# A new order of work for the first chunks, and float32 scores for four units

## The chip, the cores and the metric

The kernel runs on one core of a Trainium2 chip. The metric is the device time of one execution in microseconds. The core has TensorE (matrix multiplies, PE in the profile, its weight loads PEld), VectorE (DVE), ScalarE (ACT), GpSimd (POOL) and SyncE (SP), which here issues every DMA. Each engine has its own stream of instructions, works through it in order, and waits for the others by semaphores.

## The reference

Causal attention with a window of 64 keys, batch 8, 8 heads, 576 positions, head dimension 64, and behind it a gated feed-forward layer over the 4608 tokens, 512 wide, with 2048 hidden units, in float32:

```python
scores = scale * np.matmul(q, k.transpose(0, 1, 3, 2))
mask = (rel >= 0) & (rel < window)
scores = np.where(mask, scores, -1000000000.0)
attn = np.exp(scores - np.max(scores, axis=-1, keepdims=True))
attn = attn / (np.sum(attn, axis=-1, keepdims=True) + 1e-09)
x = np.matmul(attn, v)                  # (4608, 512) after the heads are joined
h = x @ w_in
sp = np.maximum(h, 0.0) + np.log1p(np.exp(-np.abs(h)))
return (h * erf(sp)) @ w_out
```

`w_in` and `w_out` arrive in float64, 8 MB each, and are seen as pairs of int32.

## The kernel before

**Precision.** A float32 matrix is split into a float16 high part and a float16 rest, both scaled by a power of two, and a product is three float16 matmuls: high by high, high by rest, rest by high. The power of two comes from the largest exponent of the data: of q, k and v per chunk, of a weight per pair of tiles.

**Tiles.** The tokens form 36 *units* of 128 and 18 *chunks* of two units. The hidden layer is cut in two halves, so there are 36 *groups*, each one chunk with one half of the weights; `ORDER` (L42) says which, and before the change groups 0 to 3 are chunk 0 with both halves, then chunk 1 with both. The weights come in 16 raw tiles of 1 MB, 0 to 7 from `w_in`, 8 to 15 from `w_out`; tiles 0 to 3 and 8 to 11 belong to the first half. `SLOTS` (L44) says in which buffer a raw tile lands: two staging buffers, two buffers of the hidden layer, and the room of the second half of `w_out` (A, B) until its own values are written there.

**A unit of attention.** Load q, k, v (`lq`, `lk`, `lv`, L320 to L328); peaks of each (`pk`, L332); the chunk's scales, through two small matmuls (`pa pb px py pc`, L344 to L364); high parts and rests (`qh ql kh kl vh vl`); scores (`s`, L383: 48 matmuls of 64x64 weights); mask and row maximum on VectorE (`m`, L396), subtraction (`f`, L402), two exponentials per half of the heads on ScalarE (`e`, L406: one writes float16, one float32), the rest (`r`, L411); DMA transposes (`t`, L415); weighting of v (`a`, L418); division (`n`, L426); split (`xh`, `xl`) and transposes (`xt`) of the result.

**A weight tile.** Fetch (`L`, L464); from float64 to float32: low bits on VectorE (`d`, L474), re-biasing of the exponent on ScalarE (`c`, L478), assembly on VectorE (`o`, L482); largest value (`b`, L488); for a pair, the scale through small matmuls (`mb mx my mc`, L492 to L507) and a diagonal matrix of it (`dg`, L509); high part (`h`, L521); the rest either on VectorE (`l`, L525) or as a sum on TensorE, float32 weight by diagonal less the high part (`lp`, L531 and L532), narrowed by `le` (L438).

**A group.** Four blocks of 24 matmuls for the hidden layer (`mm`, L568), each evicted by `ev`; softplus and erf in two halves (`sp` L580, `er` L584), the product (`gt`, L588), its split (`gh`, `gl`), and the output's matmuls (`mA`, `mB`, L604), added up over the two halves in the buffer `ob` (`fo`, L607) and stored (`st`). Exponential, softplus and erf lie in different tables of ScalarE, and a change of table is an instruction (ACT_TABLE_LOAD).

**Order.** The whole program is one string, `PLAN` (L47 to L208). Each word is a call: `e:3:1` is the exponentials of unit 3, second half of the heads; a trailing `a`, `v` or `g` chooses ScalarE, VectorE or GpSimd. The words are called one after the other and nothing reorders them, so the string sets each engine's order and that of all DMA issues on SyncE. `wm:k:n` (L619) issues n matmuls of the identity into an unused corner of a PSUM bank; nobody reads them.

Of the kernel before, what the change touches and what calls it, by code (L numbers as in the profile page):

```python
# [41 lines left out]
ORDER = [(0, 0), (0, 1), (1, 0), (1, 1)]  # L42
ORDER = ORDER + [(c, hf) for c in range(len(ORDER) // 2, NCH) for hf in range(2)]
SLOTS = "S0 S1 A B h1 y1 S0 S1 A B S0 S1 S0 S1 S0 S1".split()  # L44

# [644 lines left out]
```

## Time and profile before

| | us |
|---|---|
| median of 3 runs | 951.34 |
| lowest, highest | 949.7, 952.21 |
| the profiled execution | 948.91 |
| its span, first to last instruction | 947.1 |
| TensorE busy, all matmuls | 907.8 |
| of it hidden layer (L568) | 393.3 |
| of it output (L604) | 262.5 + 136.5 |
| of it filling matmuls (L621) | 37.6 |

A profile is one execution. A row of a group of instructions reads: line, engine, operation, output <- input, shapes, count | busy time in all, mean of one in ns | idle time of the engine just before them, and what ended it. A row of the timeline starts with its start and its length in us. A row of the stretches gives the length, the busy time of each engine in it with the number of instructions, TensorE's granted clock as a share of full speed, the busy share of the DMA engines and GB/s.

### The profile page before, as it was taken

How to read it: one execution, taken by the hardware profiler on the slowest of the kernel's cores; microseconds unless marked ns; L12 is line 12 of the kernel's file. 1: busy time of each engine (PE TensorE's matmuls, PEld its weight loads, DVE VectorE, ACT ScalarE, POOL GpSimd, SP SyncE). 2: the span in 40 equal slices, each digit the busy share in tenths (PEclk: the TensorE clock that was granted, in tenths of full speed). 3: DMA queues.
4: the chain of work that ended last, by engine and by line, in shares of the span. 5: the costliest groups of instructions: out<-in, count | busy, mean ns of one | idle time of the engine just before them, and what ended most of it. 6: DMA issues, size and time to landing. Idle time of an engine off the chain costs nothing.

```text
span 947.1 us, 22314 instructions
## 1 busy us (share of the span) xinstructions
PE 907.8 (96%) x9344; PEld 607.6 (64%) x9344; DVE 669.0 (71%) x1521; ACT 639.3 (68%) x740; POOL 291.5 (31%) x262
## 2 busy tenths in 40 slices
PE   8879898899999999999999999999999999999998
PEld 7547566656666666676766666666666666676663
DVE  4877887889879878476868686868686767644232
ACT  5878958889587785384848484848575757574543
POOL 0222243522245441424252525252525252501000
PEclk9989899999999999999999999999999999999999
DMA  9675673433443642343333334343434342402000
GB/s 367 161 194 175 161 151 87 145 99 101 129 107 107 142 111 79 59 109 78 113 76 115 79 113 89 102 96 102 99 96 92 93 101 55 77 15 33 14 23 23
DMA packets 140533, 98.64 MB, mean 104 GB/s; under 512 B 117776, under 2 KB 117904, under 8 KB 140432
## 3 DMA queue, kind: packets, MB, share of 16 engines
q1 hardware_dynamic: 140432, 97.22, 40.5%
q8 instruction: 73, 1.20, 0.5%
q14 instruction: 28, 0.23, 0.1%
HBM read 59.44 MB, written 9.44 MB: 73 GB/s over the span
## 4 chain that ended last, share of the span: by engine, by line
PE 68%; DVE 14%; DMA 9%; ACT 6%; issue 2%; SPq 1%; POOL 0%; DVEq 0%; ACTq 0%
PE o L604 38%; PE hp L568 22%; DMA vr<-v_in 5%; PE av L423 4%; DVE vs L318 3%; DVE y L588 3%; PE s L390 3%; DMA kr<-k_in 2%; DVE peaks L339 2%; DVE ob L613 1%; PE av L621 1%; ACT stage L478 1%; PE o L531 1%; ACT p L408 1%; ACT sm L409 1%
## 5 line engine op out<-in xcount | busy, mean ns | idle before, releaser
L568 PE MATMUL hp<-xt,w 128*128 128x256 f16 x3456 | 393.3, 273 | 1.3 <-ACT h L311 1.3
L568 PEld LDWEIGHTS <-w 128*128 128x128 f16 x3456 | 335.9, 98 | 53.7 <-issue 2.0
L604 PE MATMUL o<-w,gh 128*128 128x512 f16 x1152 | 262.5, 381 | 0.7 <-ACT ob L311 0.3
L604 PEld LDWEIGHTS <-gh 128*128 128x128 f16 x1152 | 109.9, 98 | 125.6 <-issue 3.2
L311 ACT ACTIVATE h<-hp,c 128x512 f32<-128x512 f32 x76 | 51.4, 679 | 138.4 <-PE hp L568 138.3
L604 PE MATMUL o<-w,gl 128*128 128x512 f16 x576 | 136.5, 380 | 0.0
L318 DVE SCALAR_TENSOR_TENSOR gl<-y,sg,gh 128x1024 f16<-128x1024 f32 x72 | 93.1, 1294 | 26.3 <-PE o L604 24.0
L311 ACT ACTIVATE gh<-y,sg 128x1024 f16<-128x1024 f32 x67 | 76.7, 1145 | 48.2 <-DVE y L588 30.1
L404 POOL TENSOR_TENSOR sm<-sm,mx 128x512 f32<-128x512 f32 x41 | 46.5, 1138 | 189.1 <-DVE mx L399 188.2
L413 POOL TENSOR_TENSOR p<-sm,p 128x512 f16<-128x512 f32 x63 | 78.6, 1248 | 66.0 <-ACT sm L409 62.8
L588 DVE TENSOR_TENSOR y<-h,y 128x1024 f32<-128x1024 f32 x72 | 86.8, 1224 | 13.2 <-ACT y L584 13.2
L313 DVE TENSOR_SCALAR h<-hp,c 128x512 f32<-128x512 f32 x68 | 50.5, 744 | 55.8 <-PE hp L568 53.6
L446 POOL TENSOR_TENSOR xs<-x,xs 128x512 f16<-128x512 f32 x33 | 52.7, 1597 | 119.0 <-DVE xs L440 87.4
L604 PEld LDWEIGHTS <-gl 128*128 128x128 f16 x576 | 52.8, 98 | 54.8
L408 ACT ACTIVATE p<-sm,shift,cde 128x512 f16<-128x512 f32 x72 | 58.2, 808 | 36.5 <-POOL sm L404 32.4
L399 DVE CUSTOM_DVE_ANT_0 sm<-s,mask 128x128 f32<-128x128 f32 x288 | 65.0, 285 | 19.6 <-POOL p L413 10.5
L315 POOL TENSOR_SCALAR qs<-qr,csc 128x512 f16<-128x512 f32 x28 | 29.8, 1074 | 149.8 <-DVE csc L306 136.2
L580 ACT ACTIVATE y<-h 128x1024 f32<-128x1024 f32 x72 | 72.9, 1050 | 2.1 <-DVE gl L318 1.5
L584 ACT ACTIVATE y<-y 128x1024 f32<-128x1024 f32 x72 | 73.0, 1050 | 0.4
L409 ACT ACTIVATE sm<-sm,shift,cde 128x512 f32<-128x512 f32 x72 | 58.6, 814 | 2.4
L318 DVE SCALAR_TENSOR_TENSOR vs<-vr,csc,vs 128x1024 f16<-128x1024 f32 x36 | 54.0, 1527 | 3.0 <-POOL vs L315 3.0
L613 DVE SCALAR_TENSOR_TENSOR ob<-o,sg,ob 128x512 f32<-128x512 f32 x36 | 26.3, 745 | 41.9 <-PE o L604 41.8
(129 smaller groups left out, 984.1 us busy)
## 6 DMA issues: line engine op xcount, KB each, us to landing
vr<-v_in SPq DMA_DIRECT2D x36, 512.0 KB, 4.6
kr<-k_in SPq DMA_DIRECT2D x36, 384.0 KB, 3.7
qr<-q_in SPq DMA_DIRECT2D x36, 256.0 KB, 2.8
out<-ob SPq DMA_DIRECT2D x36, 256.0 KB, 2.3
stage<-w_out SPq DMA_DIRECT2D x6, 1024.0 KB, 5.3
stage<-w_in SPq DMA_DIRECT2D x4, 1024.0 KB, 5.4
w<-w_in SPq DMA_DIRECT2D x2, 1024.0 KB, 10.9
w<-w_out SPq DMA_DIRECT2D x2, 1024.0 KB, 6.7
```

What stands on the lines that cost most here:

```text
L311: nc.scalar.activation(dst, src, AF.Copy, scale=s)
L318: nc.vector.scalar_tensor_tensor(dst, src, s, hi, op0=ALU.mult, op1=ALU.subtract)
L399: nc.vector.tensor_tensor_reduce(smi(u, par)[:, j, :], sps[par][:, j, :], mask[:, var, :], 1.0, LOWEST, op0=ALU.add, op1=ALU.max, accum_ou ...
L408: nc.scalar.activation(pp[0][u % 2][:, HP * par:HP * par + HP, :], s, AF.Exp, bias=shift14, scale=es)
L409: nc.scalar.activation(s, s, AF.Exp, bias=shift14, scale=es)
L413: eng_of(eng).tensor_tensor(pp[1][u % 2][:, sl, :], smi(u, par), pp[0][u % 2][:, sl, :], op=ALU.subtract)
L446: eng_of(eng).tensor_tensor(xs[1][u % 2], x_flat(u), xs[0][u % 2], op=ALU.subtract)
L568: nc.tensor.matmul(hps[pc % 2][:, f, :], w1[a][:, cc, fs], xt[b][c % 2][:, cc, :], start=(n == 0), stop=(n == 3 * NCC - 1))
L580: nc.scalar.activation(at(yb, g, n), at(hb, g, n), AF.Softplus)
L584: nc.scalar.activation(y, y, AF.Erf)
L588: nc.vector.tensor_tensor(y, at(hb, g, n), y, op=ALU.mult)
L604: nc.tensor.matmul(ops[j], a[:, f, ts], w2[b][:, hf * GF + f, :], start=f == 0 and a is gh and b == 0, stop=f == GF - 1 and a is gl)
```

## The change

- `PLAN` is new up to chunk 8's first hidden blocks; behind that the engines' orders are those of before. There is no `wm` in it (570 matmuls less), and `warm` and the unused `table` are gone. The attention of unit 0 stands first, ahead of the weights.
- `ORDER`: groups 0 to 3 are now chunks 0 and 1 with the first half, then both with the second half. Weight tiles 0 to 3 and 8 to 11 are treated first, 4 to 7 and 12 to 15 later. Two output buffers (`ob`) hold the sums of chunks 0 and 1 meanwhile.
- `SLOTS` has two more places, C and D, in the room of `w_in`'s second half, where the tile lies in four pieces of 256 values (two DMAs), so the raw tile gets two more dimensions everywhere.
- Scores of units 0 to 3 are float32 matmuls of q and k as loaded, 16 instead of 48, with the constant 0.125 as the exponentials' scale. Their `qh ql kh kl` and the peaks of q and k are gone; v keeps its own.
- `mA` and `mB` are split by the output's 128 rows (a fourth field), the same matmuls in the same number.

```diff
-ORDER = [(0, 0), (0, 1), (1, 0), (1, 1)]
+ORDER = [(0, 0), (1, 0), (0, 1), (1, 1)]
-SLOTS = "S0 S1 A B h1 y1 S0 S1 A B S0 S1 S0 S1 S0 S1".split()
+SLOTS = "S0 S1 A B S0 S1 A B C D h1 y1 S0 S1 S0 S1".split()
+RAW = 4
+XT_BUFS, OB_BUFS = 2, 2
...
-    "wm:0:207 L:0 L:1 L:2 L:3 lq:0 lk:1 L:4 lm lv:0 lk:0 lq:1 lv:1 L:5 d:0 c:0 o:0 d:1 b:0:a c:1 d:2 o:1 c:2 b:1:a "
+    "lk:0 lq:0 lm s:0 lv:1 m:0:0 lq:1 lv:0 pk:1:2:v f:0:0:g e:0:0 L:0 m:0:1 f:0:1:g pk:0:2:v e:0:1 r:0:0:v lk:1 L:1 "
...
-    ob = ring("ob", 1, [P, TPC, DM])
+    ob = ring("ob", OB_BUFS, [P, TPC, DM])
...
     def scores(u):
+        terms = ((0, 0), (0, 1), (1, 0))
+        if u < RAW:
+            terms = ((None, None),)
         for i in range(HP):
-            for n, (a, b) in enumerate(((0, 0), (0, 1), (1, 0))):
+            for n, (a, b) in enumerate(terms):
+                qx, kx = (qr[u % 2], kr[u % 2]) if a is None else (qs[a][u % 2], ks[b][u % 2])
...
-                        nc.tensor.matmul(sps[par][t, i, :], qs[a][u % 2][rows, i, t],
-                                         ks[b][u % 2][rows, i, W * blk:W * blk + P], start=n == 0, stop=n == 2)
+                        nc.tensor.matmul(sps[par][t, i, :], qx[rows, i, t], kx[rows, i, W * blk:W * blk + P],
+                                         start=n == 0, stop=n == len(terms) - 1)
...
     def expo(u, par):
         s, es = smi(u, par), cde[u // TPC][:, 1:2]
+        if u < RAW:
+            es = 0.125
...
+    slots["C"], slots["D"] = (w1[n][:, :, DF // 2:].bitcast(I32).rearrange("p (a b) n -> p a b n", b=2) for n in range(2))
...
-    def mm2(g, n, terms):
+    def mm2(g, n, j, terms):
...
-    def warm(k, n):
-        for _ in range(n):
-            nc.tensor.matmul(idle, ident, ident[:, :120], start=True, stop=True)
```

How the change moves instructions, at three places. First SyncE, the head of its stream; `stage`, `w2` and `h1` are the places of raw weight tiles, `kr`, `qr`, `vr` the loaded k, q, v of even (0) and odd (1) units. Before:

```order
L470 DMA stage0_148<-w_in 128x2x1024
L470 DMA stage1_149<-w_in 128x2x1024
L470 DMA w2_0_139<-w_in 128x2x1024
L470 DMA w2_1_140<-w_in 128x2x1024
L321 DMA qr0_99<-q_in 128x512
L324 DMA kr1_102<-k_in 128x768
L470 DMA h1_142<-w_in 128x2x1024
L330 DMA mask_61<-mask_in 128x384
L327 DMA vr0_103<-v_in 128x1024
L324 DMA kr0_101<-k_in 128x768
```

and of the change:

```order
L338 DMA kr0_101<-k_in 128x768
L335 DMA qr0_99<-q_in 128x512
L344 DMA mask_61<-mask_in 128x384
L341 DMA vr1_104<-v_in 128x1024
L335 DMA qr1_100<-q_in 128x512
L341 DMA vr0_103<-v_in 128x1024
L495 DMA stage0_149<-w_in 128x2x1024
L338 DMA kr1_102<-k_in 128x768
L495 DMA stage1_150<-w_in 128x2x1024
L495 DMA w2_1_140<-w_in 128x2x1024
L436 DMA_TRANSPOSE pt0_0_124<-p0_0_120 128x8x128
```

k, q and v of units 0 and 1 have moved ahead of the weight tiles, and the first transpose of unit 0's weights (`pt`) now stands behind the third weight tile.

Second ScalarE, the head of its stream; L478 is the re-biasing of a weight tile, L488 its largest value, L337 a peak of k; in the change L428 and L429 are the exponentials, L503 the re-biasing, L325 here the high part of v, L513 the largest value. Before:

```order
L478 ACT_TABLE_LOAD
L478 ACTIVATE stage0_148<-stage0_148 128x1024
L488 ACTIVATE stage0_148,acc_63<-stage0_148 128x1024
L478 ACTIVATE stage1_149<-stage1_149 128x1024
L478 ACTIVATE w2_0_139<-w2_0_139 128x1024
L488 ACTIVATE stage1_149,acc_63<-stage1_149 128x1024
L337 ACTIVATE junk_84,peaks_62<-kr1_102 128x768
L478 ACTIVATE w2_1_140<-w2_1_140 128x1024
```

and of the change:

```order
L428 ACT_TABLE_LOAD
L428 ACTIVATE p0_0_120<-sm0_117,shift14_64 128x512
L429 ACTIVATE sm0_117<-sm0_117,shift14_64 128x512
L428 ACTIVATE p0_0_120<-sm1_118,shift14_64 128x512
L429 ACTIVATE sm1_118<-sm1_118,shift14_64 128x512
L503 ACTIVATE stage0_149<-stage0_149 128x1024
L503 ACTIVATE stage1_150<-stage1_150 128x1024
L325 ACTIVATE vs0_0_113<-vr0_103,csc_77 128x16x64
L325 ACTIVATE vs0_1_114<-vr1_104,csc_77 128x16x64
L513 ACTIVATE stage0_149,acc_63<-stage0_149 128x1024
L513 ACTIVATE stage1_150,acc_63<-stage1_150 128x1024
```

Four exponentials of unit 0 have moved to the front, where the first weight tile stood, and the peaks of k are gone.

Third ScalarE just ahead of its first instruction that serves the hidden layer (`h0<-hp`) in the program before, and ahead of the narrowing of the last weight sum that TensorE has queued before its first hidden matmul in the change. L438 (L458) with `w1_1` is a narrowing, with `xs` the attention's result. Before:

```order
L438 ACTIVATE xs0_1_130<-x0_128 128x512
L311 ACTIVATE qs0_1_106<-qr1_100,csc_77 128x512
L311 ACTIVATE qs0_0_105<-qr0_99,csc_77 128x512
L311 ACTIVATE vs0_1_114<-vr1_104,csc_77 128x16x64
L311 ACTIVATE vs0_0_113<-vr0_103,csc_77 128x16x64
L438 ACTIVATE w1_1_138<-o0_155 128x512
L478 ACTIVATE w2_1_140<-w2_1_140 128x1024
L438 ACTIVATE w1_1_138<-o1_156 128x512
L488 ACTIVATE w2_1_140,acc_63<-w2_1_140 128x1024
L311 ACTIVATE h0_141<-hp0_153,c1_89 128x512
```

and of the change:

```order
L513 ACTIVATE w1_1_138,acc_63<-w1_1_138 128x4x256
L428 ACTIVATE p0_0_120<-sm1_118,shift14_64 128x512
L429 ACTIVATE sm1_118<-sm1_118,shift14_64 128x512
L458 ACTIVATE w1_1_138<-o1_157 128x512
L503 ACTIVATE y1_144<-y1_144 128x1024
L458 ACTIVATE w1_1_138<-o0_156 128x512
L458 ACTIVATE w1_1_138<-o1_157 128x512
L503 ACTIVATE h1_142<-h1_142 128x1024
```

In the change re-biasings of `w_out` tiles (L503 on `y1`, `h1`) and exponentials stand between the narrowings; the one into `w1_1` from `o0` frees the buffer in which TensorE's last sum ahead of its first hidden matmul is made.

More of the change, by code (lines that the diff above doesn't have):

```diff
@@ L268, in window_attention_gated_ffn @@
     xs = [ring(f"xs{n}_", 2, [P, DM], F16) for n in range(2)]
-    xt = [ring(f"xt{n}_", 2, [P, NCC, CT], F16) for n in range(2)]
+    xt = [ring(f"xt{n}_", XT_BUFS, [P, NCC, CT], F16) for n in range(2)]
     w1 = ring("w1_", 2, [P, NCC, DF], F16)
@@ L283, in window_attention_gated_ffn @@
     wrow, wall = avb[:1, 1, row_at:row_at + P], avb[:, 1, row_at + P:row_at + P + 1]
-    idle = avb[:, 0, row_at + P + 3:row_at + P + 123]
     hps = [ps.tile([P, 2, CT], F32, name=f"hp{i}") for i in range(2)]
@@ L449, in x_turn @@
         c, j = divmod(u, TPC)
-        nc.sync.dma_start_transpose(out=xt[n][c % 2][:, :, j * P:(j + 1) * P], in_=xs[n][u % 2])
+        nc.sync.dma_start_transpose(out=xt[n][c % XT_BUFS][:, :, j * P:(j + 1) * P], in_=xs[n][u % 2])
     slots = {"h0": hb[0], "h1": hb[1], "y0": yb[0], "y1": yb[1], "S0": stage[0], "S1": stage[1]}
-    slots = {n: t.bitcast(I32) for n, t in slots.items()}
-    slots["O"] = None
-    slots["A"], slots["B"] = (w2[n][:, GF:].rearrange("p f e -> p (f e)").bitcast(I32) for n in range(2))
+    slots["A"], slots["B"] = (w2[n][:, GF:].rearrange("p f e -> p (f e)") for n in range(2))
+    slots = {n: t.bitcast(I32).rearrange("p (a b n) -> p a b n", a=2, b=2) for n, t in slots.items()}
+    slots["C"], slots["D"] = (w1[n][:, :, DF // 2:].bitcast(I32).rearrange("p (a b) n -> p a b n", b=2) for n in range(2))
     def raw_tile(u):
@@ L460, in raw @@
     def raw(u):
-        r = raw_tile(u).rearrange("p (n w) -> p n w", w=2)
-        return r[:, :, 0], r[:, :, 1]
+        r = raw_tile(u).rearrange("p a b (n w) -> p a b n w", w=2)
+        return r[:, :, :, :, 0], r[:, :, :, :, 1]
     def fetch(u):
@@ L469, in fetch @@
             src = w_out[2 * (u - 8) * P:2 * (u - 7) * P, :]
-        nc.sync.dma_start(raw_tile(u).rearrange("p (a b) -> p a b", a=2), src.rearrange("(c p) f -> p c f", p=P))
+        dst = raw_tile(u)
+        if SLOTS[u] in "CD":
+            for a in range(2):
+                nc.sync.dma_start(dst[:, a], src[a * P:(a + 1) * P, :].rearrange("p (b f) -> p b f", b=2))
+        else:
+            nc.sync.dma_start(dst.rearrange("p a b n -> p a (b n)"), src.rearrange("(c p) f -> p c f", p=P))
     def low_bits(u):
@@ L489, in bound @@
         else:
-            nc.vector.tensor_reduce(dst, lo, axis=AX.X, op=ALU.max, apply_absolute_value=True)
+            nc.vector.tensor_reduce(dst, lo, axis=AX.XYZ, op=ALU.max, apply_absolute_value=True)
     def pair_rows(j):
@@ L512, in parts @@
         j = u // 2
-        t = raw(u)[0].bitcast(F32).rearrange("p (c n) -> p c n", c=2)
+        t = raw(u)[0].bitcast(F32)
         if u < 8:
@@ L519, in parts, with quarters @@
         return t, sw2[:, j - 4:j - 3], hi, lo
+    def quarters(x):
+        return x.rearrange("p c (b n) -> p c b n", b=2)
     def high(u, eng):
         t, s, hi, _ = parts(u)
-        scaled(eng, hi, t, s)
+        scaled(eng, quarters(hi), t, s)
     def low(u):
         t, s, hi, lo = parts(u)
-        rest(lo, t, s, hi)
+        rest(quarters(lo), t, s, quarters(hi))
     def low_sum(u, a):
         t, _, hi, _ = parts(u)
-        nc.tensor.matmul(ops[a], diag[u // 2 % 2], t[:, a], start=True, stop=False)
+        nc.tensor.matmul(ops[a].rearrange("p (b n) -> p b n", b=2), diag[u // 2 % 2], t[:, a], start=True, stop=False)
         nc.tensor.matmul(ops[a], minus, hi[:, a], start=False, stop=True)
@@ L567, in mm1 @@
                 for a, b in ((0, 0), (0, 1), (1, 0)):
-                    nc.tensor.matmul(hps[pc % 2][:, f, :], w1[a][:, cc, fs], xt[b][c % 2][:, cc, :], start=(n == 0),
+                    nc.tensor.matmul(hps[pc % 2][:, f, :], w1[a][:, cc, fs], xt[b][c % XT_BUFS][:, cc, :], start=(n == 0),
                                      stop=(n == 3 * NCC - 1))
@@ L595, in g_lo @@
         rest(glb[:, sl], at(yb, g, n), st_g[g][:, n:n + 1], ghb[:, sl])
-    def mm2(g, n, terms):
+    def mm2(g, n, j, terms):
         hf = ORDER[g][1]
         gh, gl = (t.rearrange("p (f t) -> p f t", t=CT) for t in (ghb, glb))
-        for j in range(TPC):
-            ts = slice(j * P, (j + 1) * P)
-            for f in range(n * GF // 2, (n + 1) * GF // 2):
-                for a, b in (((gh, 0), (gh, 1)) if terms == 0 else ((gl, 0),)):
-                    nc.tensor.matmul(ops[j], a[:, f, ts], w2[b][:, hf * GF + f, :],
-                                     start=f == 0 and a is gh and b == 0, stop=f == GF - 1 and a is gl)
+        ts = slice(j * P, (j + 1) * P)
+        for f in range(n * GF // 2, (n + 1) * GF // 2):
+            for a, b in (((gh, 0), (gh, 1)) if terms == 0 else ((gl, 0),)):
+                nc.tensor.matmul(ops[j], a[:, f, ts], w2[b][:, hf * GF + f, :],
+                                 start=f == 0 and a is gh and b == 0, stop=f == GF - 1 and a is gl)
     def result(g, j, eng="v"):
@@ L617, in store @@
         nc.sync.dma_start(out[r0:r0 + P, :], ob[c % len(ob)][:, j, :])
-    def warm(k, n):
-        for _ in range(n):
-            nc.tensor.matmul(idle, ident, ident[:, :120], start=True, stop=True)
-    def table(n):
-        nc.scalar.preload_act_table_set(("exp_and_others", "softplus", "sigmoid_and_others")[n])
     HANDLERS = {
@@ L632, in window_attention_gated_ffn @@
         "W": w_in_scale, "V": w_out_scale, "dc": descale, "gn": gains, "mm": mm1, "ev": hidden,
-        "sp": softplus, "er": erf, "gt": gate, "gh": g_hi, "gl": g_lo, "mA": lambda g, n: mm2(g, n, 0),
-        "mB": lambda g, n: mm2(g, n, 1), "fo": result, "st": store, "T": table, "wm": warm,
+        "sp": softplus, "er": erf, "gt": gate, "gh": g_hi, "gl": g_lo, "mA": lambda g, n, j: mm2(g, n, j, 0),
+        "mB": lambda g, n, j: mm2(g, n, j, 1), "fo": result, "st": store,
     }
```

329 rows, old and new, of the table PLAN are left out of this document.

## The prediction, made before the changed kernel was run

> **What bounds the kernel now.** I read the busy table first, then the busy time of each engine in stretches, then the timeline of TensorE.
>
> ```profile
> PE 907.8 (96%) x9344; PEld 607.6 (64%) x9344; DVE 669.0 (71%) x1521; ACT 639.3 (68%) x740; POOL 291.5 (31%) x262
> ```
>
> The span is 947.1 us and TensorE is busy for 96% of it, so over the whole program it is the bound. That figure contains the filling matmuls, so the next view cuts the span at three matmuls that stand out in the timeline: the first hidden-layer matmul (71.32), the first of group 4, which is chunk 2 with the first half of the weights (163.60), and the third pair of group 16, chunk 8 (476.49).
>
> ```profile
> 71.32 5.40 PE L568 MATMUL hp<-xt,w 128*128 128x256 f16 x48
> 163.60 5.42 PE L568 MATMUL hp<-xt,w 128*128 128x256 f16 x48
> 476.49 2.79 PE L568 MATMUL hp<-xt,w 128*128 128x256 f16 x24
> ```
>
> ```profile
> core 0: us, PE busy (x) PEld busy (x) DVE busy (x) ACT busy (x) POOL busy (x), PEclk, DMA share, GB/s
> 0.00:71.32 71.32, 56.34 (x767) 41.17 (x768) 49.00 (x119) 50.26 (x70) 15.55 (x30) 0.95 0.77 240
> 71.32:163.60 92.28, 80.80 (x958) 58.90 (x955) 72.92 (x170) 74.80 (x98) 29.35 (x27) 0.94 0.55 139
> 163.60:476.49 312.89, 309.31 (x3153) 202.67 (x3145) 248.99 (x579) 226.35 (x258) 112.61 (x95) 1.00 0.43 108
> 476.49:947.10 470.61, 461.37 (x4486) 304.87 (x4478) 298.05 (x655) 287.92 (x316) 133.95 (x110) 1.00 0.32 74
> ```
>
> The same stretches for the filling matmuls (L621) alone, PE first:
>
> ```profile
> 0.00:71.32 71.32, 32.90 (x519) 30.80 (x519) 0.95 0.77 240
> 71.32:163.60 92.28, 4.66 (x54) 3.99 (x51) 0.94 0.55 139
> ```
>
> The ledger of TensorE up to 476.49 is then: busy 56.34 + 80.80 + 309.31 = 446.45, of it filler 32.90 + 4.66 = 37.56, so **408.9 us of work**, and 476.49 - 408.9 = **67.6 us without work** (48 before the first hidden matmul, 16 up to 163.60, 4 after). From 163.60 on it hardly waits. In the first 163.6 us ScalarE is busy for 125 and VectorE for 122, three quarters of it: the weights' conversion and the first attention units run through these two, and TensorE waits for their chain.
>
> Behind 476.49 the two kernels have the same instructions in the same order on TensorE (only the two row halves of one group's output are named apart), so the 470.6 us that follow stay. The question is how much of the 67.6 us goes.
>
> **The change part by part.** *Work removed and added.* Four units lose the float16 split of q and k and its peaks: on VectorE eight residuals and four peaks, on ScalarE four peaks and most of the scalings.
>
> ```profile
> L318 DVE SCALAR_TENSOR_TENSOR ks<-kr,csc,ks 128x768 f16<-128x768 f32 x36 | 41.6, 1186 | 0.1
> L318 DVE SCALAR_TENSOR_TENSOR qs<-qr,csc,qs 128x512 f16<-128x512 f32 x36 | 26.8, 775 | 0.1
> L339 DVE TENSOR_REDUCE peaks<-qr 128x1 f32<-128x512 f32 x31 | 20.7, 679 | 0.9 <-DMA qr<-q_in 0.9
> L580 ACT ACT_TABLE_LOAD x40 | 51.3, 1283 | 4.3 <-DVE cpw L360 3.6
> ```
>
> 4 x (1.186 + 0.775 + 0.679) = 10.6 us leave VectorE. ScalarE gains: its order now has 122 table loads for 105, 17 x 1.283 = 21.8 us, nearly all before chunk 8. By counts times these rows, ScalarE has some 11 us more ahead of the cut at 476.49, where it was idle for 125 us; it is hidden as long as ScalarE is not the late one, which it is only up to chunk 1 (below).
>
> *The float32 scores.* No score in float32 is in the trace. A float32 matmul of 512 columns is (L531), and a float16 one (L604), and the float16 scores (L390):
>
> ```profile
> 160.48 1.07 PE L531 MATMUL o<-stage,diag 128*128 128x512 f32 x2
> 161.39 0.38 PE L532 MATMUL o<-w,minus 128*128 128x512 f16 x1
> 122.40 0.86 PE L390 MATMUL s<-ks,qs 64*64 64x128 f16 x48
> 123.20 3.63 PE L604 MATMUL o<-w,gh 128*128 128x512 f16 x16
> 126.76 0.86 PE L390 MATMUL s<-ks,qs 64*64 64x128 f16 x48
> ```
>
> 161.39 - 160.48 = 0.91 us against (126.76 - 123.20) / 16 = 0.22: 4.1 times. 48 float16 score matmuls took 0.80; 16 in float32 at 4.1 times are 1.1 us if the four 64x64 corners still run side by side, and 16 x 0.91 / 4 = 3.6 us if they do not. Per unit +0.3 to +2.8, for four units +1 to +11. I take **+2**, near the scores' own row; all four stand ahead of the first hidden matmul or just there, where TensorE waits anyway. If that cover is gone it costs the whole.
>
> *The first stretch.* Now the loads of weights go first, and k waits behind them; the first softmax exponential starts at 36.79.
>
> ```profile
> 3.75 0.50 SPq L324 DMA_DIRECT2D kr<-k_in  x1
> 16.49 0.84 ACT L337 ACTIVATE junk<-kr 128x768 uint8<-128x768 f32 x1 [2.40 <-DMA kr<-k_in]
> 36.79 0.81 ACT L408 ACTIVATE p<-sm,shift,cde 128x512 f16<-128x512 f32 x1
> kr<-k_in SPq DMA_DIRECT2D x36, 384.0 KB, 3.7
> ```
>
> After the change k and q of unit 0 are the first two loads: at 3.7 us behind an issue at about 1 they land near 5, the scores end near 7, two masked maxima and a shift follow, and the first exponential starts near 10. From there ScalarE has, ahead of what the first hidden matmul needs, 6 pairs of exponentials, 7 re-biasings (L478), 6 bounds (L488), 2 scalings of v, 2 of weights, 4 narrowings (L438) and 2 diagonals:
>
> ```profile
> L408 ACT ACTIVATE p<-sm,shift,cde 128x512 f16<-128x512 f32 x72 | 58.2, 808 | 36.5 <-POOL sm L404 32.4 <-DVE sm L404 3.9
> L409 ACT ACTIVATE sm<-sm,shift,cde 128x512 f32<-128x512 f32 x72 | 58.6, 814 | 2.4
> L478 ACT ACTIVATE stage<-stage 128x1024 f32<-128x1024 f32 x10 | 11.4, 1138 | 3.9 <-DMA stage<-w_in 3.9
> L488 ACT ACTIVATE stage<-stage 128x1024 f32<-128x1024 f32 x9 | 10.4, 1157 | 4.5 <-DVE stage L482 4.4
> L488 ACT ACTIVATION_READ_ACCUMULATOR stage<-stage 128x1 f32 x9 | 1.8, 199 | 0.0
> L311 ACT ACTIVATE vs<-vr,csc 128x1024 f16<-128x1024 f32 x4 | 4.4, 1136 | 0.0
> L311 ACT ACTIVATE w<-stage,sw 128x1024 f16<-128x1024 f32 x4 | 4.8, 1212 | 0.0
> L438 ACT ACTIVATE w<-o 128x512 f16<-128x512 f32 x14 | 8.1, 596 | 1.6 <-PE o L532 1.6
> L509 ACT ACTIVATE diag<-unit,sw 128x128 f32<-128x128 f32 x8 | 3.2, 398 | 2.9 <-DVE sw L306 2.9
> ```
>
> 6 x 1.62 + 7 x 1.14 + 6 x 1.36 + 2 x 1.14 + 2 x 1.21 + 4 x 0.60 + 2 x 0.40 = 33.7 us. VectorE has 34 of its own. So nothing starts before 10 + 33.7 = 44, and the two hand work to each other in order: a weight tile goes VectorE, ScalarE, VectorE, ScalarE, and followed by hand through the rows above ScalarE stands three times before a re-biasing whose low-bits step is queued on VectorE behind attention (2 + 1 + 4 us), the last just ahead of the narrowing (the third piece of order in the section on the change) that the first hidden matmul waits for. With smaller gaps the first hidden matmul comes at **53 us**. Ends: 43 without a wait; 58 where ScalarE is busy for the same 70% (50.26 of 71.32) as before. TensorE's work ahead of it: now 56.34 - 32.90 = 23.4 with as many low-part sums and scores a few tenths longer, but one sum less per weight tile still open: 21. So **without work 53 - 21 = 32** (22 to 37) for 48.
>
> *First hidden matmul to chunk 1's (group 1).* ScalarE has in this part of the order 5 re-biasings, 4 bounds, 6 narrowings, 2 pairs of exponentials, 3 hidden evictions, 2 softplus and 2 erf, each with a table load, and 7 smaller pieces:
>
> ```profile
> L311 ACT ACTIVATE h<-hp,c 128x512 f32<-128x512 f32 x76 | 51.4, 679 | 138.4 <-PE hp L568 138.3
> L580 ACT ACTIVATE y<-h 128x1024 f32<-128x1024 f32 x72 | 72.9, 1050 | 2.1 <-DVE gl L318 1.5
> ```
>
> 5.7 + 5.4 + 3.6 + 3.2 + 2.0 + 4 x (1.05 + 1.28) + 6.6 = 36 us, of which some 4 us are not needed for group 1's first matmul. In these 31 us TensorE has 26 of work (4 hidden blocks at 5.42 / 2, 6 weight sums at 1.1, 4 weighings at 0.5, 3 quarter blocks of the output at 1.8, small ones): 5 without work (2 to 14). From there to the cut TensorE has work at every step I followed up to group 2; but VectorE, 80% busy between 163.60 and 476.49 (248.99 of 312.89), gets work that was done earlier: by counts times rows it is 82 us between the starts of groups 4 and 8, or 77, since such a sum over the whole program stands 7% above the 669.0 of the busy table; TensorE needs 83 there, so VectorE is at 93%. I take 7 without work (4, as now, to 14, that is 77 / 0.80 = 96 less 83). Together 12 for 20.
>
> *The filler.* It leaves 37.6 us of busy time that were no work, so its going costs nothing by itself. What it covered is the clock. TensorE's granted clock (the column behind POOL) falls when it was idle:
>
> ```profile
> 60.00:64.00 4.00, 1.12 (x16) 0.80 (x15) 2.65 (x12) 2.02 (x3) 2.59 (x3) 1.00 1.23 281
> 64.00:68.00 4.00, 2.72 (x17) 1.57 (x18) 2.89 (x9) 2.38 (x4) 1.60 (x2) 0.55 0.34 66
> 68.00:72.00 4.00, 4.00 (x17) 2.02 (x16) 3.07 (x5) 3.30 (x5) 0.00 (x0) 0.59 0.10 10
> 72.00:76.00 4.00, 4.00 (x39) 3.60 (x37) 1.96 (x3) 1.12 (x2) 0.00 (x0) 1.00 0.92 362
> ```
>
> After 4 us with 1.12 busy the clock is 0.55, and it is back after some 4 us of busy time. Without filler TensorE has 21 us of work in 53, so it will mostly run at about 0.55 there. Most of that stretches work into waits; on the chain are a few sums and the first hidden matmuls: 4 us at 0.57 lose 3. I take **+3** (0 to 20; the 408.9 already hold the slow stretches of now).
>
> The Trainium skill, in "TensorE: Matmul & The Clock Gate", Part 1, says the same as a rule that speaks against this change: a window of about 3.4 us without activity halves the clock, and another busy one is needed to restore it. The trace agrees (0.55 behind 1.12 busy in 4.00); taken over the whole first 100 us it is the last rival below, and by the 3 us above it would only be paid once or twice.
>
> *SyncE.* The transposes of the first units now stand between weight loads, which so wait for the first exponentials (about 15 us); the loads ahead of that point are 5.7 MB, 24 us at the first stretch's 240 GB/s, so the DMA engines are not out of work before. The second output buffer (`ob`) frees the accumulation from its store; no wait of TensorE in the page is put down to a store, so 0.
>
> **The sum.** 408.9 + 2 (scores) + 32 + 12 + 3 (clock) = 457.9 for 476.49: **18.6 us less**. The profiled execution took 948.91 (1.8 around its span): 930.3. The median of the runs shown is 951.34, 2.4 above it, so 932.7; I say **932 us**.
>
> **The rivals.** *It goes better*: ScalarE and VectorE hardly wait for each other. Then the low ends hold: 408.9 + 1 + 22 + 6 + 0 = 437.9, and the time is 951.34 - 38.6 = 913. For it: four units need no chunk scale ahead of their scores, and the second halves of the weights are not due before group 2, so each engine has more to choose from. Against: in the first 163.6 us ScalarE has held no more than 125. **0.20.**
>
> *It is only moved*: in-order queues give the gain back, since softplus and erf of chunks 0 and 1 and the second halves of the weights now meet in the same stretch with chunk 2 and 3's attention. With the high ends of the waits, 37 + 14 + 14, and the clock's 3: 408.9 + 2 + 65 + 3 = 478.9, the time 954; with one of them a little lower no change, 943 to 954. For it: VectorE's 93% between groups 4 and 8. **0.13.**
>
> *The clock stays down*, which ends slower. Place: from the first hidden matmul to group 2, about 51 us of TensorE's work, with short gaps by weight sums. If the gaps keep the granted clock at 0.57 there, it takes 51 / 0.57 - 51 = 38 longer, of which the 5 of waiting hide some: 457.9 + 33 = 491, the time **966**. It decides from a mean clock below 51 / (51 + 18.6 + 5) = 0.68 in that stretch; at 0.8 it costs 8 and the change is still faster. Against: between 71.32 and 163.60, with 4.66 of filler, the clock was 0.94. **0.10.**
>
> **How the numbers follow.** Forecast 0.57, better 0.20, moved 0.13, clock 0.10. A measurement of this kernel tells about 0.3%, 2.9 us, from no change. Faster: 0.57 + 0.20 + 0.05 of the third = 0.82; same 0.06; slower 0.10 + 0.02 = 0.12. The forecast's own range is 918 to 943; to leave out no more than 2 in 10 the range reaches down to the better case, 910, and up to the third, 950.
>
> **What would show it.** First exponential near 10 us and first hidden matmul near 53 (43 to 58); TensorE without work before it about 32 us; first matmul of group 1 near 85; the third pair of group 16 near 458, and 470 us behind it. A granted clock near 0.55 before 55 us and above 0.8 from there to 110. Wrong would be: a first hidden matmul later than 65, TensorE idle for over 10 us between groups 4 and 8 behind VectorE, or score matmuls of over 3 us a unit.

## The result, and the profile after

| | before | after |
|---|---|---|
| median of 4 runs each, us | 951.78 | 918.64 |
| lowest, highest, us | 949.7, 952.39 | 916.71, 918.84 |
| profiled execution, us | 948.91 | 918.84 |
| its span, us | 947.1 | 917.1 |

The ratio is 0.9651, with a 95% interval of 0.9631 to 0.9671: 33 us, 3.5%, faster. The forecast said 932, between 910 and 950; the direction and the range held, and the gain came out larger than its 19 us.

The busy table of the changed kernel:

```profile
PE 872.6 (95%) x8710; PEld 574.7 (63%) x8710; DVE 673.4 (73%) x1513; ACT 647.7 (71%) x738; POOL 274.0 (30%) x251
```

TensorE's share is lower by one point although the kernel is faster: 37.6 us of filler are gone from it. What counts is again the time without work, so here is the same cut. (The 16 float32 score matmuls of a unit are recorded as 32.) The timeline of TensorE gives the places: the first scores, the first hidden-layer matmul, that of group 1 (now chunk 1 with the first half), and the row that holds the third pair of group 16 as its second half.

```profile
4.64 1.99 PE L408 MATMUL s<-kr,qr 64*64 64x128 f32 x32 [4.64 <-DMA qr<-q_in]
...
39.99 1.10 PE L408 MATMUL s<-kr,qr 64*64 64x128 f32 x32
...
47.84 5.72 PE L596 MATMUL hp<-xt,w 128*128 128x256 f16 x48
...
75.94 5.74 PE L596 MATMUL hp<-xt,w 128*128 128x256 f16 x48 [0.28 <-DMA xt<-xs]
...
438.65 5.40 PE L596 MATMUL hp<-xt,w 128*128 128x256 f16 x48
```

24 such matmuls take 2.62 from start to start (484.50 - 481.88 further on), so the cut lies at 438.65 + 2.62 = 441.27. The stretches (length, busy time of PE, PEld, DVE, ACT, POOL, granted clock, DMA share, GB/s); 161.51 is a hidden-layer matmul of group 4:

```profile
0.00:47.84 47.84, 22.17 (x259) 12.70 (x260) 35.66 (x122) 34.24 (x47) 18.14 (x31) 0.97 1.04 315
47.84:161.51 113.67, 109.72 (x969) 67.55 (x967) 100.40 (x181) 98.48 (x121) 42.70 (x35) 1.00 0.50 143
161.51:441.27 279.76, 277.35 (x3014) 189.07 (x3007) 236.96 (x565) 223.68 (x250) 74.25 (x67) 1.00 0.45 107
441.27:917.10 475.83, 463.40 (x4480) 305.34 (x4477) 300.36 (x649) 291.29 (x322) 138.91 (x120) 0.99 0.33 78
```

Up to the cut TensorE is busy for 22.17 + 109.72 + 277.35 = 409.24 us, all of it work, and without work for 25.67 + 3.95 + 2.41 = 32.0, where it was 67.6. The cut comes 476.49 - 441.27 = **35.2 us earlier**. Behind it the same instructions take 475.83 instead of 470.61: **5.2 us are given back**. 35.2 - 5.2 = 30.0 is the difference of the two spans (947.1 - 917.1); the medians differ by 3 more.

### The profile page after: what moved, and what is told of

The parts are those of the page before. It is cut to its first block, busy times and chain, and to the rows that moved or that the text cites. A ratio compares the mean times of both kernels' runs of the same rounds, so it can differ in the third digit from the quotient of the medians.

```text
span 917.1 us, 20949 instructions
## 1 busy us (share of the span) xinstructions
PE 872.6 (95%) x8710; PEld 574.7 (63%) x8710; DVE 673.4 (73%) x1513; ACT 647.7 (71%) x738; POOL 274.0 (30%) x251
## 4 chain that ended last, share of the span: by engine, by line
PE 66%; DVE 16%; DMA 9%; issue 3%; ACT 2%; POOL 1%; SPq 1%; DVEq 0%; POOLq 0%; ACTq 0%
PE o L631 34%; PE hp L596 25%; DMA vr<-v_in 5%; DVE vs L332 3%; PE av L443 3%; DVE y L616 2%; PE s L408 2%; DVE peaks L353 2%; DVE sm L417 1%; DMA stage<-w_in 1%; DMA w<-w_out 1%; DMA w<-w_in 1%; PE o L559 1%; DVE gl L332 1%; DVE sm L422 1%
## 5 line engine op out<-in xcount | busy, mean ns | idle before, releaser
L631 PE MATMUL o<-w,gh 128*128 128x512 f16 x1152 | 265.9, 381 | 0.7 <-ACT ob L325 0.5
L631 PE MATMUL o<-w,gl 128*128 128x512 f16 x576 | 139.8, 380 | 0.2 <-DVE gl L332 0.2
L325 ACT ACTIVATE h<-hp,c 128x512 f32<-128x512 f32 x82 | 55.3, 677 | 104.0 <-PE hp L596 103.8
L332 DVE SCALAR_TENSOR_TENSOR gl<-y,sg,gh 128x1024 f16<-128x1024 f32 x72 | 95.4, 1326 | 19.2 <-PE o L631 17.8
L433 POOL TENSOR_TENSOR p<-sm,p 128x512 f16<-128x512 f32 x54 | 68.8, 1276 | 83.7 <-ACT sm L429 79.1
L422 POOL TENSOR_TENSOR sm<-sm,mx 128x512 f32<-128x512 f32 x37 | 42.7, 1156 | 170.8 <-DVE mx L417 170.8
L325 ACT ACTIVATE gh<-y,sg 128x1024 f16<-128x1024 f32 x55 | 62.9, 1144 | 40.2 <-DVE y L616 30.8
L428 ACT ACTIVATE p<-sm,shift,cde 128x512 f16<-128x512 f32 x64 | 51.9, 810 | 42.5 <-POOL sm L422 29.8
L327 DVE TENSOR_SCALAR h<-hp,c 128x512 f32<-128x512 f32 x62 | 45.9, 744 | 47.1 <-PE hp L596 46.6
L466 POOL TENSOR_TENSOR xs<-x,xs 128x512 f16<-128x512 f32 x27 | 40.9, 1516 | 109.1 <-DVE xs L460 49.5
```

What stands on the lines that cost most here:

```text
L325: nc.scalar.activation(dst, src, AF.Copy, scale=s)
L327: nc.vector.tensor_scalar(dst, src, s, None, op0=ALU.mult)
L332: nc.vector.scalar_tensor_tensor(dst, src, s, hi, op0=ALU.mult, op1=ALU.subtract)
L422: eng_of(eng).tensor_tensor(s, s, m.unsqueeze(2).broadcast_to([P, HP, P]), op=ALU.subtract)
L428: nc.scalar.activation(pp[0][u % 2][:, HP * par:HP * par + HP, :], s, AF.Exp, bias=shift14, scale=es)
L433: eng_of(eng).tensor_tensor(pp[1][u % 2][:, sl, :], smi(u, par), pp[0][u % 2][:, sl, :], op=ALU.subtract)
```

## The experiments

Twelve kernels were run, each beside runs of the kernel before on the same chip; these gave medians of 951.1 to 951.4, beside the change 951.78, so the times below are set side by side. In what follows "end" is the difference of medians; the interval of a ratio is about 0.002 on either side, so differences under 3 us between two of these kernels don't settle anything alone.

### The parts of the change, one at a time

**Before without its filler.** All `wm` words are left out, nothing else.

```diff
-    "wm:0:207 L:0 L:1 L:2 L:3 lq:0 lk:1 L:4 lm lv:0 lk:0 lq:1 lv:1 L:5 d:0 c:0 o:0 d:1 b:0:a c:1 d:2 o:1 c:2 b:1:a "
+    "L:0 L:1 L:2 L:3 lq:0 lk:1 L:4 lm lv:0 lk:0 lq:1 lv:1 L:5 d:0 c:0 o:0 d:1 b:0:a c:1 d:2 o:1 c:2 b:1:a "
```

> The kernel before with its 570 filling matmuls taken out and nothing else changed. My theory: the filler is no work and its going frees nothing, but it kept TensorE at full clock; without it the weight sums, scores and the first hidden matmuls up to about 100 us run at half speed, so the time is 3 to 10 us longer, first hidden matmul near 74 to 80 us. Rival (the changed kernel gains by losing the filler's 37.6 us of TensorE time): 5 to 35 us shorter. Rival (the clock is worth nothing there): within 2 us.

Measured: 946.89 for 951.17, ratio 0.9948 (0.9932 to 0.9965), 4.3 us **faster**. The theory fell, and the number lies between the two rivals. Its stretch up to the first hidden matmul, and that matmul:

```profile
0.00:69.24 69.24, 30.57 (x249) 12.95 (x249) 49.62 (x118) 49.28 (x69) 14.43 (x30) 0.83 0.75 246
69.24 5.40 PE L566 MATMUL hp<-xt,w 128*128 128x256 f16 x48
```

The clock did fall (0.83 for 0.95), and TensorE's work grew from 23.4 to 30.6 us; yet the first hidden matmul comes 2.1 us earlier than 71.32. So the stretched work lies mostly in waits, while a filling matmul that stands in TensorE's order ahead of work whose data are there holds it up. The timeline of before has one such place just at the end, five fillers ahead of a first hidden matmul that waits for nothing else; they are 0.46 of the 2.1 us:

```profile
70.86 0.62 PE L621 MATMUL av<-ident 128*128 128x120 bf16 x5
71.32 0.93 PE L568 MATMUL hp<-xt,w 128*128 128x256 f16 x7
```

Which of the 570 held up what was not tried one by one. The two spans (947.1 and 943.6) differ by 3.5 us, 1.9 of it at the cut; the other 1.6 arise behind it, where neither kernel has filler.

**The changed kernel with filler.** 278 of the same matmuls in nine places where TensorE waits (`warm` is put back), for instance

```diff
-    "lk:0 lq:0 lm s:0 lv:1 m:0:0 lq:1 lv:0 pk:1:2:v f:0:0:g e:0:0 L:0 m:0:1 f:0:1:g pk:0:2:v e:0:1 r:0:0:v lk:1 L:1 "
+    "lk:0 lq:0 lm wm:0:40 s:0 lv:1 m:0:0 lq:1 lv:0 pk:1:2:v f:0:0:g e:0:0 L:0 m:0:1 f:0:1:g pk:0:2:v e:0:1 r:0:0:v "
```

> The changed kernel with 278 filling matmuls put into the waits of TensorE in the first 46 us, each some 80% of the wait it stands in. If the clock was the cost there: float32 scores of units 0 to 2 take 1.1 us instead of 2.0, the first weight sums 0.9 instead of 1.9, the first hidden matmul comes 1 to 4 us before 47.84, and the time is 1 to 4 us shorter. If the half speed only stretched work into waits: within 1 us. If filler behind which other work queues is late: 1 to 3 us longer.

Measured: 922.51, ratio 0.9702 (0.968 to 0.9725), 3.9 us **slower** than the change. The third expectation came, a little larger. The first scores are quick now, but start later, and so does the first hidden matmul:

```profile
5.99 1.10 PE L409 MATMUL s<-kr,qr 64*64 64x128 f32 x32
...
49.18 5.72 PE L597 MATMUL hp<-xt,w 128*128 128x256 f16 x48
```

In both orders filler costs about 4 us at the end, whatever it saves in clock, and the change gains by leaving it out. How the loss comes about is shown only in part: here 1.3 of the 5.1 us between the spans are there at the first hidden matmul, and the rest arises behind the last filler.

**Float32 scores in the old order.** A first attempt left the loads of q and k of unit u+2 ahead of unit u's scores, so that these read q and k of a later unit and waited for their load.

> The kernel before with float32 scores for units 0 to 3, their splits and the peaks of q and k left out, order otherwise as it was. My theory: what the float32 scores are worth is that unit 0 no longer waits for a chunk scale, and that only pays where attention stands first; in the old order some 10 us of VectorE and 7 us of ScalarE work go, of which a part is on the chain: 2 to 7 us shorter. Rival (the work removed is the gain): 10 to 18 us shorter. Rival (nothing, it is hidden): within 2 us.

Measured: 951.88, ratio 1.001 (0.9992 to 1.0028). Since the scores waited for loads that they don't need, it settles nothing; in the second attempt the loads stand behind the scores:

```diff
-pc:0 lp:1:0 wm:5:35 d:5 qh:0:a qh:1:v kh:0:a ql:0 c:5 kl:0 lq:2 ql:1 s:0 wm:6:34 lk:2 o:5
+pc:0 lp:1:0 wm:5:35 d:5 c:5 s:0 lq:2 wm:6:34 lk:2 o:5
...
+        if u < 4:
+            terms = ((None, None),)
```

> The kernel before, in its old order, with one part of the change: the first four units' scores come from float32 q and k, so that the peaks and the float16 splits of q and k of those units are gone, and the load of unit u+2's q and k stands behind unit u's scores. Theory (the order carries the gain; in the old order the splits lie beside weight work that the first hidden matmul waits for anyway): 2 to 7 us shorter than before, first hidden matmul 2 to 6 us earlier than the 71 of before. Rival (the removed VectorE and ScalarE work is itself the gain): 10 to 18 us shorter. Rival (float32 scores are worth nothing): within 2 us.

Measured: 952.68, ratio 1.0019 (1.0004 to 1.0034). Nothing is gained, which is the second rival. The stretch up to its first hidden matmul:

```profile
0.00:70.75 70.75, 56.03 (x736) 41.94 (x736) 40.45 (x106) 43.97 (x58) 12.54 (x28) 0.90 0.75 242
```

VectorE has 8.6 us less in it than before (40.45 for 49.00) and ScalarE 6.3 less (43.97 for 50.26), and TensorE's first hidden matmul moves by 0.57. So in the old order neither engine's amount of work set that place.

**The change without float32 scores for units 0 and 1.** Their peaks, scales and float16 splits are back, their loads first:

```diff
-    "lk:0 lq:0 lm s:0 lv:1 m:0:0 lq:1 lv:0 pk:1:2:v f:0:0:g e:0:0 L:0 m:0:1 f:0:1:g pk:0:2:v e:0:1 r:0:0:v lk:1 L:1 "
+    "lk:0 lq:0 lk:1 lq:1 lv:0 lv:1 lm L:0 L:1 L:3 pk:0:1:a pk:0:0:v pk:1:1:a pk:1:0:v pk:0:2:v pk:1:2:v pa:0 pb:0 "
+    "px:0 py:0 pc:0 qh:0:a kh:0:v ql:0 kl:0 s:0 m:0:0 f:0:0:g e:0:0 m:0:1 f:0:1:g e:0:1 r:0:0:v d:0 c:0 c:1 qh:1:a "
...
-        if u < RAW:
+        if 1 < u < RAW:
```

> The changed kernel, but units 0 and 1 go back to float16 halves of q and k with a chunk's scale (peaks, scale, splits and three matmuls a block), their loads first. Theory (the float32 scores buy the early start of the exponentials): first exponential at 16 to 20 us instead of 8.7, first hidden matmul 6 to 10 us later, the end 6 to 10 us later than the changed kernel. Rival (the early stretch is bound by the weights' loads and their splits, the exponentials have slack): 0 to 3 us later.

Measured: 928.6, ratio 0.9772 (0.9746 to 0.9798), 10.0 us slower than the change. Its first exponential (timeline of ScalarE) beside that of the change:

```profile
19.29 0.81 ACT L429 ACTIVATE p<-sm,shift,cde 128x512 f16<-128x512 f32 x1 [5.27 <-POOL sm L423]
```

```profile
8.74 0.72 ACT L428 ACTIVATE p<-sm,shift 128x512 f16<-128x512 f32 x1 [6.72 <-POOL sm L422]
```

19.3 for 8.7, the first transpose of unit 0's weights issued at 21.68 for 11.47, and the first hidden matmul at 57.80, 10 us later than 47.84. The theory held: float32 scores are worth 0 in the old order (four units) and 10 us in the new one (two of them), where the first exponential stands at the head of everything.

### What sets the first hidden matmul now

My forecast took ScalarE's queue as the bound. Two engines and the loads were tried, each with work added or taken away.

**Two more loads of 1 MB** on SyncE's queue, into a hidden-layer buffer that is not yet in use:

```diff
+    def reload(u):
+        src = w_in[2 * P:4 * P, 1024:2048]
+        nc.sync.dma_start(slots["y0"].rearrange("p a b n -> p a (b n)"), src.rearrange("(c p) f -> p c f", p=P))
...
+L:1 LX:0 ... L:2 LX:0
```

> The changed kernel with two additional loads of 1 MB of w_in on SP's queue (behind the second and the fourth weight load, into a buffer that nothing reads before it is written again), 2 MB more ahead of the first hidden matmul. At the 315 GB/s that the first 48 us move, 2 MB are 6.7 us. Theory (the loads bound the stretch before the first hidden matmul): that matmul 4 to 7 us later, the end 4 to 7 us later than the changed kernel. Rival (ScalarE and VectorE bound it): end 0 to 1.5 us later.

**Four activations on ScalarE done twice** (`b:2 b:3 b:8 b:9`), 5.4 us:

> The changed kernel with four activations on ScalarE (the bounds of four weight rows) done twice, some 5.4 us more ScalarE work ahead of the first hidden matmul, results unchanged. Theory (before the first hidden matmul the VectorE and ScalarE chain is the bound): 3 to 5 us longer. Rival (the DMA queues are the bound there, at a busy share of 1.04): 0 to 1.5 us longer.

**Two reductions on VectorE done three times more** (`pk:2:2 pk:3:2`), 4.1 us:

> The changed kernel with two reductions on VectorE (half peaks of v of units 2 and 3) done three times more, some 4.1 us more VectorE work ahead of the first hidden matmul, results unchanged. Theory (VectorE and ScalarE are the bound there): 2 to 4 us longer. Rival (the DMA queues are the bound there): 0 to 1.5 us longer.

**Bounds of weight rows left out** (`b:1 b:3 b:9 b:11`):

> The changed kernel without four of the weight rows' bounds on ScalarE (three of them, 3.9 us of ScalarE, stand ahead of the first hidden matmul); the scale of those rows then comes from half of the rows. Theory (ScalarE's work bounds the stretch before the first hidden matmul): 2 to 4 us shorter than the changed kernel. Rival (the loads bound it): within 1 us.

**Work of the first two `w_out` tiles behind the first hidden matmuls.**

```diff
-d:8 c:8 o:8 b:8:a c:9 d:9 o:9 b:9:a c:11 ... mb:4 mx:4 my:4 mm:0:0 mc:4 ... mm:0:1
+mm:0:0 d:8 c:8 o:8 b:8:a c:9 d:9 o:9 b:9:a c:11 ... mm:0:1 mb:4 mx:4 my:4 mc:4
```

> The changed kernel with the integer work and bounds of the first two w_out tiles (9 words of the plan, some 8 us of ScalarE and 6 us of VectorE) behind the first hidden matmuls of group 0 instead of ahead of them; all loads stay where they were. Theory (VectorE and ScalarE set the first hidden matmul): that matmul 5 to 8 us earlier, the end 2 to 6 us earlier, the rest being given back where the moved work now stands. Rival (the loads of w_in set it): the first hidden matmul within 2 us of where it was, the end 0 to 4 us later.

| | first hidden matmul, us | median, us | ratio to before (95%) |
|---|---|---|---|
| the change | 47.84 | 918.64 | 0.9651 (0.9631, 0.9671) |
| 2 MB more to load | 51.90 | 922.06 | 0.9692 (0.9675, 0.971) |
| 5.4 us more on ScalarE | 50.51 | 920.27 | 0.9682 (0.9661, 0.9702) |
| 4.1 us more on VectorE | 51.74 | 919.2 | 0.9675 (0.965, 0.9701) |
| three bounds less on ScalarE | 47.80 | 915.72 | 0.9632 (0.9609, 0.9655) |
| 7 us of ScalarE, 4 of VectorE moved behind | 47.77 | 922.24 | 0.9697 (0.968, 0.9713) |

The stretches of these kernels bear the edits out, for instance 31.40 us of ScalarE for 34.24 with three bounds less. The last two rows are the clear ones. Here is the moved version, its stretch up to the first hidden matmul, then TensorE's timeline:

```profile
0.00:47.77 47.77, 21.43 (x255) 12.13 (x255) 31.46 (x116) 27.03 (x36) 19.95 (x31) 1.00 1.06 313
```

```profile
47.77 5.72 PE L596 MATMUL hp<-xt,w 128*128 128x256 f16 x48 [1.17 <-DMA xt<-xs]
...
58.66 0.16 PE L525 MATMUL av<-wtop,ones 1*128 1x1 bf16 x1 [4.04 <-DVE wtop L522]
...
83.22 5.40 PE L596 MATMUL hp<-xt,w 128*128 128x256 f16 x48
```

ScalarE has 27.03 instead of 34.24 us ahead of that matmul and VectorE 31.46 instead of 35.66, and it starts at the same place. Its own row says what it waits for there: `xt`, the transposes of the attention's result. The moved work then stands on the way to group 1, which begins at 83.22 instead of 75.94, and 3.6 us of that last to the end. The last that the transposes need is the rest of unit 1's result (L466, timeline of VectorE), here in the change and then with 2 MB more to load:

```profile
41.11 0.69 DVE L466 TENSOR_TENSOR xs<-x,xs 128x512 f16<-128x512 f32 x1
```

```profile
45.18 0.69 DVE L466 TENSOR_TENSOR xs<-x,xs 128x512 f16<-128x512 f32 x1
```

In the moved version it starts at 41.15. In the change and in all eight kernels made from it, the first hidden matmul comes 5.65 to 7.02 us behind this row, so what sets it, as far as these rows show, is the attention of unit 1 with its transposes (in the change itself the last weight sum, at half speed, ends at that place as well, so its row names no wait). With 2 MB more the delay enters still earlier, at the transposes of unit 0's weights, for which TensorE waits before it weights v, again in the change and then with the loads:

```profile
26.48 1.53 PE L443 MATMUL av<-vs,pt 128*64 128x65 f16 x46 [0.71 <-DMA pt<-p]
```

```profile
30.71 1.54 PE L443 MATMUL av<-vs,pt 128*64 128x65 f16 x46 [4.98 <-DMA pt<-p]
```

This is 4.2 us later, and the first hidden matmul is 4.1 us later. So the loads are on the path through the transposes, which stand between them in SyncE's order. The chain of waits of the change names loads as well, two of 8.84 us among its longest pieces:

```profile
3.55 8.84 DMA stage<-w_in
...
25.68 8.84 DMA w<-w_out
```

The second of these leads to work that the moved version has put behind, without effect. 2 MB more at 315 GB/s are 6.7 us; the first hidden matmul came 4.1 later, as the theory had said (4 to 7), the end 3.4, a little less. Of the expectations for the moved work the rival's is what came: first hidden matmul where it was, end 0 to 4 later. VectorE and ScalarE stand close beneath: added work came through in part (2.7 of 5.4 us and 3.9 of 4.1 at the first hidden matmul), removed work not at all. Their expectations were written for the end, where +1.6 and +0.6 are too small to tell.

Why removing gives nothing can be read where unit 1's weights are applied to v: this starts at 37.79 in the change, when VectorE has assembled a `w_out` tile (to 37.67), and at 37.80 in the moved version, where VectorE is free but TensorE has worked without a gap from 29.49 to 37.55, on scores and weight sums, the first of them at half speed. Several chains end there within a few tenths, and no run shortened two of them at once. That less work on ScalarE made the end 2.9 us earlier has another cause, which the next part shows.

The Trainium skill, in "Perfetto Trace Analysis", section Roofline, bounds what a single core moves by its 16 DMA engines at about 435 GB/s. The trace agrees: the busiest slice of 4 us that I looked at moved 419.

```profile
12.00:16.00 4.00, 1.05 (x15) 0.88 (x19) 3.08 (x6) 1.40 (x3) 1.16 (x1) 1.00 1.02 419
```

### The 5 us that were given back

Behind the cut TensorE waits at one kind of place: the small matmul that spreads a chunk's peaks (`pb`, L363; L349 before) stands ahead of 16 output matmuls that don't need it. The waits of TensorE behind the cut (in all, times, longest), before and after:

```profile
PE av L349 <- DVE cmx L303: 5.1, 6, 1.2
```

```profile
PE av L363 <- DVE cmx L317: 7.5, 7, 2.8
```

The longest, with what follows it, in the change and in the kernel with fewer bounds, which has the same instructions here:

```profile
474.64 0.22 PE L363 MATMUL av<-ident,cmx 128*3 128x128 bf16 x1 [2.79 <-DVE cmx L317]
474.79 5.31 PE L631 MATMUL o<-w,gh 128*128 128x512 f16 x16
```

```profile
473.70 0.22 PE L363 MATMUL av<-ident,cmx 128*3 128x128 bf16 x1 [1.20 <-DVE cmx L317]
473.85 3.63 PE L631 MATMUL o<-w,gh 128*128 128x512 f16 x16
```

The wait is longer by 1.6 us, and behind it the same 16 matmuls take 1.7 us more, because the clock fell (column behind POOL):

```profile
476.00:480.00 4.00, 4.00 (x13) 1.40 (x11) 1.34 (x2) 3.95 (x5) 0.00 (x0) 0.68 0.00 0
```

The peaks are not waiting for TensorE. On VectorE the first of them waits for the load of v, here in the change and then in the kernel with fewer bounds:

```profile
470.76 0.69 DVE L353 TENSOR_REDUCE peaks<-vr 128x1 f32<-128x512 f32 x1 [3.71 <-DMA vr<-v_in]
```

```profile
469.82 0.69 DVE L353 TENSOR_REDUCE peaks<-vr 128x1 f32<-128x512 f32 x1 [1.71 <-DMA vr<-v_in]
```

The two are 0.9 apart, in the other direction than the cuts: the changed kernel has its cut at 441.27 against 442.72, but SyncE issues this load at 465.79 in both, and in the change it took longer to land. So there TensorE is early and the load is not. That is no rule: with 2 MB more to load, the cut lies 4.2 us later than in the change, and TensorE waits 2.93 at this place. What decides when the load lands was not settled. In these profiles the kernel with fewer bounds is 1.45 us later at the cut and 3.3 us earlier at its end (913.8); its gain comes from here, not from ScalarE's work ahead of the first hidden matmul.

**The matmuls of the chunk's scale behind the output matmuls**, for chunks 11 to 17:

```diff
-gl:16:0 pb:11 mA:16:0:0 mA:16:0:1 ev:17:3:a px:11 sp:17:1 gl:16:1 py:11 mB:16:0:0 mB:16:0:1
+gl:16:0 mA:16:0:0 mA:16:0:1 pb:11 ev:17:3:a sp:17:1 gl:16:1 px:11 mB:16:0:0 mB:16:0:1 py:11
```

> The changed kernel with the small matmuls of the chunk scale (exponent rows, then the broadcast) of chunks 11 to 17 moved behind the first output matmuls that now stand behind them, and VectorE's step between them one place later. Theory: the 7.5 us that TensorE waits there behind the cut at 441 us (the longest, 2.8 us, at 474.6, and the half clock after it, some 2 us) are waits of an instruction standing too early in the queue, for a peak of v that no output matmul needs; 5 to 9 us shorter than the changed kernel (910 to 914). Rival (VectorE or the v load is the real bound there, the wait only moves to the next instruction that needs it): within 2 us.

Measured: **912.6**, ratio 0.9588 (0.9561 to 0.9615), 6.0 us faster than the change and the fastest of all that ran. The waits at L363 are gone from behind the cut; the largest that is left there:

```profile
PE o L630 <- ACT gh L324: 1.4, 1, 1.4
```

**The same edit in the kernel before**, chunks 9 to 17:

> The kernel before with the three matmul places of the chunk scale of chunks 9 to 17 moved behind the output matmuls, as in the changed kernel's earlier run that gained 6 us by it. Theory (this wait is in both kernels, and the change made it only a little longer): 3 to 6 us shorter than before, the rows' waits behind the cut (5.1 us in the kernel before) gone. Rival (it is a loss that the change brought): within 1.5 us of before.

Measured: 946.11 for 951.13, ratio 0.9942 (0.9921 to 0.9964): 5.0 us faster, about the 5.1 us of waits. So most of this wait was there already; what the change added is one long wait and the half clock behind it.

## Why the prediction was right, and where its sizes were off

By its own sum, in us of the profiled execution:

| term | forecast | measured | off by |
|---|---|---|---|
| TensorE's work to the cut, scores and clock | 408.9 + 2 + 3 = 413.9 | 409.24 | -4.7 |
| without work before the first hidden matmul | 32 | 25.67 | -6.3 |
| without work from there to the cut | 5 + 7 = 12 | 3.95 + 2.41 = 6.4 | -5.6 |
| behind the cut | 470.6 | 475.83 | +5.2 |
| sum | 928.5 | 917.1 | -11.4 |

That the range held is in part luck: up to the cut the sum was 16.6 us too high, and 5.2 us in the other direction behind it hide a third of that. 918.64 is at the lower edge of the forecast's own 918 to 943, and nearer to the 913 of "It goes better" than to 932.

- **What bounds the kernel** held: the work to the cut is the same to within a few tenths, and the gain is time without work, 67.6 to 32.0.
- **The first exponential** was put near 10 and came at 8.74. **The scores** were put at 1.1 us a unit and took 1.03 at full clock (39.99 to the next matmul at 41.02), so the four corners do run side by side; the first three units took 1.99, 1.99 and 1.98, at half speed.
- **The first hidden matmul** is the mis-sized term: 53 forecast, 47.84 measured, within its bounds. From the first exponential on the forecast has 33.7 us of ScalarE's work and 9.3 of waits; measured were 33.0 (34.24 less the table load) and 6.1, and the start was 1.3 earlier. The step that failed is the waits of 2 + 1 + 4 us before re-biasings whose low-bits step is late on VectorE. The waits of ScalarE around and behind its first exponential were these (in all, times, longest; the 6.7 of the first row lies ahead of it):

```profile
ACT p L428 <- POOL sm L422: 7.2, 2, 6.7
ACT stage L503 <- DMA stage<-w_in: 2.6, 2, 2.4
ACT stage L513 <- DVE stage L507: 0.6, 1, 0.6
ACT w L458 <- DVE kw L317: 0.6, 1, 0.6
ACT h L503 <- DMA h<-w_out: 0.6, 1, 0.6
ACT w L325 <- DVE w L507: 0.5, 1, 0.5
ACT w L503 <- DMA w<-w_out: 0.2, 1, 0.2
ACT w L458 <- PE o L560: 0.2, 1, 0.2
```

  No re-biasing (L503) waits for VectorE, only for loads: in the kernel it and the low-bits step work on different words of the raw tile, and each needs the load alone. And although the sum of ScalarE's work was right, moving 7 us of it away changed nothing: the bound that I had not written down is the attention's transposes among the loads. I looked at 5.7 MB of loads, ahead of one point, and asked only whether the DMA engines run dry; their busy share was 1.04 over the whole stretch.
- **The clock and the filler**: +3 had the wrong sign. The clock did stay down at first (last section), but that time lay in waits: behind the half-speed sums TensorE still waited 0.78 us for VectorE at 37.79. And filler was not free: it cost 4 us in each order. "Its going costs nothing by itself" was half of it: its going gains.
- **From the first hidden matmul to the cut** I feared VectorE at 93% between groups 4 and 8 and took 7 us; 2.4 were lost. The row of L363 has 1.6 us of it. VectorE's total did not fall by the 10.6 us either, it rose from 669.0 to 673.4, because the new order gives it other work (17 of the high parts `gh` for 5).
- **Behind the cut** "the 470.6 us stay" was wrong by 5.2: the waits at L363 take 2.4 us more (7.5 for 5.1), a wait for an eviction 0.6, the half clock 1.7. The same order of instructions isn't the same time where it waits for loads that another queue issues. The kernel with fewer bounds has 471.1 there (913.8 - 442.72).
- **The rivals.** "It goes better" put the cut at 437.9; at 441.27 it is nearer to that than to the forecast's 457.9, and only the 5 us behind pull the end towards 932. "Only moved" and "the clock stays down" did not come: the mean clock from 47.84 to 161.51 was 1.00. The Trainium skill's rule in "TensorE: Matmul & The Clock Gate", Part 1, is that a window of about 3.4 us without activity halves the clock; the traces show the half clock behind less: 0.63 from 44 to 48 behind gaps of 1.38 and 1.26 us, 0.68 from 476 to 480 behind one of 2.79, and the 0.55 that the forecast showed behind gaps of 1.81 and 1.07.

Of the 33 us, the runs put some 4 on the filler and 10 on the float32 scores of units 0 and 1, the latter only together with the new order. If these two add up, which no run shows, the other 19 or so belong to the rest: the order, and with it the first half of the weights first. Order and halves were not tried apart, because the halves can't be undone without writing the order anew.

## What to carry to other kernels

Removed work is worth what the chain behind it can use: float32 scores gave nothing where weights stood ahead of them and 10 us where they stood at the head, so cost such an edit in the new order, not in the old one. When an engine's count of work seems to bound a start-up, count the bytes ahead of the same point as well, by the highest rate the trace shows, and look which transposes stand between them. And put small matmuls that wait for another engine behind the large ones that don't: 5 to 6 us here, in both kernels, for a move of words in an order.
